# Scoring all four experts in batches 4 and 5 and in one tile of batch 3, with stores on two queues and a new order

## The chip, the cores and the metric

The kernel runs on one core of a Trainium2 chip. The metric is the device time of one execution in microseconds (us), as the median of three runs. Engines are TensorE (PE, with its weight loads PEld), VectorE (DVE), ScalarE (ACT), GpSimd (POOL) and SyncE (SP), which issues the transfers.

## What is computed

The reference has two stages. The first is an attention between x (8 batches, 8 heads, 512 rows, 64 columns) and a state of 32 rows a head, in both directions; its result is a sequence of 544 tokens of 512 columns a batch. The second is a mixture of four attention experts over that sequence, of which each token takes two:

```python
logits = x @ w_gate
topk = np.argpartition(-logits, K, axis=-1)[..., :K]      # K = 2 of E = 4
...
for e in range(E):
    q, k, v = x @ wq[e], x @ wk[e], x @ wv[e]             # 64 columns each
    scores = scale * (q @ k.transpose(0, 2, 1))
    scores = np.where(causal, -1000000000.0, scores)
    scores = scores - scores.max(-1, keepdims=True)
    a = np.exp(scores)
    a /= a.sum(-1, keepdims=True) + 1e-09
    ye = a @ v @ wo[e]
    for kk in range(K):
        mask = topk[:, :, kk] == e
        out += mask[..., None] * w[:, :, kk:kk + 1] * ye
```

## The kernel before

Each float32 operand is split into a high and a low float16 half, and each product is made of three matmuls (high by high, high by low, low by high: `PROD`). The 512 tokens of a batch are four tiles of 128 (`T = 4`); the 32 state tokens of two batches together form a `tail`. For each batch, `front(b)` computes the first stage, the keys, the values, the gate and the queries; `probs(b, unit)` computes scores and exponentials of a unit, which is a list of tiles with a way of scoring; `reads(b, i)` multiplies the probabilities of tile i with the values, weights them, and `result` multiplies with `wo` and stores the tile.

There are two ways of scoring a tile. In the way `"s"` a query tile is multiplied with a mask for each of two slots, so that each slot holds the one expert that its token chose among three; `qf` is the masked query, `qh` its halves, and a DMA transpose turns them into `qm`. A tile then has two lanes of scores of 128*(i+1) columns. In each lane three matmuls have 128 rows of contraction and three have 64; those of 64 rows run in pairs. `reads` makes 194 columns for each slot: three experts of 64 columns and their sums. In the ways `"d"`, `"0"` and `"1"` no mask is used: all four experts are scored, two for each half of the pair index, so a tile has four lanes, and all its matmuls have 64 rows and run in pairs. `"d"` takes both pairs in one unit, `"0"` and `"1"` take one each. `reads` makes 65 columns for each of the four experts. Where all tiles of a batch are of this kind, the queries come out of the matmul already turned and need no mask and no DMA transpose.

For every lane `masked` (DVE) adds the causal mask and takes the row maximum, ACT takes the exponential, and `split` makes the halves `ph`: the high half on ACT, POOL or DVE, the low one on POOL or DVE. A DMA transpose turns `ph` into `pt` for the reads.

Which batch is scored in which way stands in `units_of(b)`:

```python
if b < CFG["D1"]:
    units = [((0, "s"), (1, "s")), ((2, "s"),), ((3, "s"),)]
elif b < CFG["DA"]:
    units = [((1, "d"),), ((0, "s"), (2, "s")), ((3, "s"),)]
else:
    units = [((1, "d"),), ((0, "0"), (2, "0")), ((0, "1"), (2, "1")), ((3, "0"),), ((3, "1"),)]
```

Before, D1 = DA = 6: batches 0 to 5 are scored by `"s"`, batches 6 and 7 by the others. Nothing is issued in program order: each call records a step with the ways (engines) in which it can be done, and `ORDER` holds, in coded form, one order of all steps, the way of each and the slot of each buffer. `run` (line 266 is its issuing line, so nearly all instructions carry L266) issues the steps in that order. The front of a batch is mixed with the scoring and the reads of the batches before it.

Of the kernel before, what the change touches and what calls it, by code (L numbers as in the profile page):

```python
# [18 lines left out]
CFG = dict(FILL=(1.0, 1.4, 1.8, 2.2, 2.6, 3.0, 3.4, 3.8, 4.2, 4.6,), RA=-1, RG=1, RV=2, RK=2, ZL=3, GP=1, PT=4, ZM=4, SM=4, QM=4, SIDE=32, FB=1, PX=1, PA=2, LB=1, xn=4, W0=-33, PACE=37.0, XP=(1,), QP=(0,), LAG=2,
           FRONT=1.5, FSPAN=1.0, TSPAN=1.3, TOFF=1.2, KT=3, p32=3, ph=2, at=1, et=1, gs=1, xh=4, a2=1, o=4, sn=1, qf=2,  # L20
           n_eb=1, n_e2=1, n_a2t=1, n_xt_tail=2, n_z32=3, n_z=2, n_zh=2, n_tq=1, n_tv=2, n_tpt=1, n_tz=1, n_pt=3, D1=6, DA=6)
ORDER = (
    (
        "c-jrs1A7n(7(n6AU$tu4EiBu{vTfV87nW_?wr$(CZR6hGaGvKqfshB%K{iMNksuWmg2<2_GC~oE00kivM1(|;8=^u6%nJYr1PlTS2_X%n$6S"
        "yMazI=Nf|aluih)6V2mps@um%!9bchGBAqFgk<xmb{LUD)#1uzfRfN)S2GC(XSh&ACjlz{S(1xrE&s0AUI6SCq7s0d{s8=izhSQ~O+VMqa$A"
# [3 lines left out]
        "3B%J&h(Tjv2F!v6I1Uy=1X_&?p(HlMdk{dCF(R#pHMj(-;987CO|T{|f~t5Q9zs)m1dZ@DM5e}A3Lii-ERA*XF+73iPz(3-GYF(=_y%r48N3"
        "Z&APPmLJ5Uzy!c%w))$s+C!*}o=YG7*E$F(s#e1MnG4Zp!hsE1#nBi2WwHuwoTqf>Hdj^E)kq=j(Q4(nhi?2bKf9k#_E&;t8mZw$pg*dKpFU"  # L30
        "pxo{uqO`0$v6oA(QgXF!Pp)r;t=eGf2bvPz@ZqEUcq`ChU0M~PC(#E*achREbNL?ur;Ql88{Ua&}<xzKj<$_!<qOC5>jf~fTQvM<Q$8B!yNn"
        "zBQOmG(R7SWV{jz?1H)06mj1w8+=S_9EXJj5G!6mNQyhwk@yHP|5ydCw#551X;ZNF({U|4e$0QUB4?zSBCBmc>8-wX92{UG=WV9V~(>4^`f&"
        "ti{lAvO8%104#0R5tGl!7ARR?I{B={xPfIJgs2QZC9syKo?7q}_M`<KiC7M0sg1=Ag)U7*66o%uE|)5FNxr7)Hv6F$?YG!E_YM(-DlwS;;sW"
# [34 lines left out]
        "c-mc((YB>92tx@_`u~4CJM?%T#-+<@X-Gn<zAGvtZbY2;|58TBgcRp?B#UZSid#xeq}uy=3=%r?9WCklVDfM>Q|$U=XZm%MZHk8fQQ<DZnuY"
        "R~VJ2>KVv1TV8&+yipmpW99!nsW3liFm=wLSQp+nL~b=`;cvd^f|pH6-@pNOM)VO0<>W0$NLbNV@SI+mQj&d5HL1t4eDVd!z+!I4od#`CLj`"
        "mBz89&#-y`*N37M{DiCR~KZvfh-GE+rmb2!c8^l4GIg{2s>*nD~`w4qj76)OqXqZPNJ%8eSd>SV=W!!%7i!;c|bQku*qkeMTK!}rz5}-3ak!"  # L70
        "Uwd%IZn+^F9m|fP-V9H<mvIaIi&}9*Mjb;=xaX{)3)-hUbe9VY_=fhJs#w?gq@@XNm_t)fYI^ml_tGiAbFR+}ohhiNyxeE8}FB?0<No^|Nwu"
        "Y(S{PfF3@^kL<RZ!cS<H);`VcccgJDsyWBcbW-V6NxPuMD3X&yzE8UTWfJ){|6E_CI6E1{V"
# [1142 lines left out]
```

## Time and profile before

| what | value |
| --- | --- |
| median of three runs | 285.18 us (284.17 to 285.38) |
| the profiled execution | 284.73 us |
| its span, from first to last instruction | 283.0 us |
| granted TensorE clock, mean | 0.994 |
| busy, PE / DVE / ACT / POOL | 270.7 / 252.9 / 230.5 / 170.2 us |

The profiled execution has 1.7 us outside the span that the trace shows. Busy times count each engine's own instructions, overlaps once; a mean in nanoseconds counts the whole of one instruction, with the part that overlaps its neighbour.

### The profile page before, as it was taken

The page shows a single profiled execution, that of the slowest core. Times are in us where ns is not written, and L with a number is a line of the kernel's source. Part 1 is how long each engine was busy: PE and PEld are TensorE (multiplying, and loading weights), DVE is VectorE, ACT ScalarE, POOL GpSimd, SP SyncE. Part 2 cuts the span into 40 slices and gives each one's busy share as a digit, 9 for nine tenths or more (in the row PEclk, how much of TensorE's full clock was granted, in tenths as well). Part 3 has the DMA queues.
Part 4 walks back from the last instruction along what each step waited for, and adds up shares of the span by engine and source line. Part 5 has one row for each costly group of instructions (what it writes and reads, how often), then busy time and mean ns, then how long its engine had stood idle before and what let it go on. Part 6 is the DMA issues. An engine that isn't in the chain of part 4 may idle for free.

```text
span 283.0 us, 9152 instructions
## 1 busy us (share of the span) xinstructions
PE 270.7 (96%) x3406; PEld 182.6 (65%) x3407; DVE 252.9 (89%) x795; ACT 230.5 (81%) x624; POOL 170.2 (60%) x246
## 2 busy tenths in 40 slices
PE   8969999998998999989999999999999999999995
PEld 4757665857477664758677756668567575666763
DVE  2588999899999999999999998999998999979962
ACT  3689998899799999778988889796777698869523
POOL 7522556596784897859656974577685842654010
PEclk9979999999999999999999999999999999999999
DMA  7956799999999999995999999998788799699996
GB/s 197 237 107 157 182 195 177 195 218 171 179 173 193 145 186 292 192 201 135 238 197 183 190 201 230 141 203 209 133 152 164 226 147 199 122 184 188 209 227 244
DMA packets 161804, 53.16 MB, mean 188 GB/s; under 512 B 140640, under 2 KB 157280, under 8 KB 161760
## 3 DMA queue, kind: packets, MB, share of 16 engines
q1 hardware_dynamic: 161760, 52.59, 95.0%
q8 instruction: 26, 0.43, 0.6%
q14 instruction: 18, 0.15, 0.2%
HBM read 11.02 MB, written 8.91 MB: 70 GB/s over the span
## 4 chain that ended last, share of the span: by engine, by line
PE 68%; DVE 19%; ACT 6%; issue 3%; DMA 2%; SPq 1%; POOL 0%; DVEq 0%; ACTq 0%
PE bank L266 68%; DMA xn<-in_x_dram 2%; DVE eb L266 2%; DVE xh L266 1%; DVE qf L266 1%; DVE sbm L266 1%; DVE gs L266 1%; DVE mb L266 1%; DVE p L266 1%; DVE z L266 1%; DVE a L266 1%; DVE ph L266 1%; SPq L266 1%; DVE m L266 1%; DVE et L266 1%
## 5 line engine op out<-in xcount | busy, mean ns | idle before, releaser
L266 PE MATMUL bank<-gs,at 128*128 128x260 f16 (+3 forms) x320 | 44.8, 284 | 1.4 <-DVE kt L266 0.8
L266 ACT ACTIVATE p<-p,mx 128x256 f32<-128x256 f32 (+3 forms) x80 | 41.8, 554 | 2.8 <-DVE mx L266 1.7
L266 PE MATMUL bank<-v,pt 128*128 128x194 f16 (+1 forms) x600 | 42.1, 226 | 0.5 <-DVE mx L266 0.4
L266 PE MATMUL bank<-kt,qm 64*128 64x128 f16 (+7 forms) x384 | 42.3, 298 | 0.2 <-DVE kt L266 0.2
L266 PEld LDWEIGHTS <-pt 128*128 128x128 f16 x600 | 38.3, 97 | 5.2 <-issue 2.9
L266 DVE CUSTOM_DVE_ANT_0 p<-bank,band 128x384 f32<-128x384 f32 (+3 forms) x80 | 36.4, 481 | 0.7 <-PE bank L266 0.3
L266 POOL TENSOR_TENSOR ph<-p,ph 128x1024 f16<-128x1024 f32 (+1 forms) x17 | 32.8, 1930 | 5.7 <-ACT ph L266 5.1
L266 PEld LDWEIGHTS <-at 128*128 128x128 f16 x288 | 27.3, 97 | 9.3 <-issue 2.9
L266 PEld LDWEIGHTS <-qm 64*128 64x128 f16 (+1 forms) x384 | 21.0, 95 | 17.1 <-issue 7.6
L266 PE MATMUL bank<-at,gs 128*128 128x512 f16 (+1 forms) x116 | 29.3, 395 | 0.7 <-ACT gs L266 0.7
L266 PE MATMUL bank<-wo_n,z 128*128 128x512 f16 (+1 forms) x114 | 26.2, 368 | 0.0
L266 ACT ACTIVATE ph<-p 128x1024 f16<-128x1024 f32 (+1 forms) x21 | 20.3, 965 | 0.4
L266 POOL TENSOR_TENSOR qh<-qf,qh 128x768 f16<-128x768 f32 x10 | 17.1, 1719 | 4.9 <-ACT qh L266 4.9
L266 PE MATMUL bank<-wo_n,zp 128*128 128x512 f16 x84 | 19.9, 379 | 0.0
L266 ACT ACTIVATE o<-bank 128x512 f32<-128x512 f32 (+1 forms) x27 | 15.4, 575 | 4.9 <-PE bank L266 2.7
L266 DVE SCALAR_TENSOR_TENSOR xh<-xn,xh 128x512 f16<-128x512 f32 x26 | 18.3, 705 | 0.0
L266 POOL TENSOR_TENSOR eb<-eb,sbm 128x512 f32<-128x512 f32 x14 | 15.1, 1077 | 5.1 <-DVE gt L266 2.4
L266 PEld LDWEIGHTS <-gs 128*128 128x128 f16 x108 | 10.2, 98 | 11.5 <-issue 1.1
L266 PEld LDWEIGHTS <-xh 128*128 128x128 f16 x416 | 14.4, 99 | 4.1 <-DVE xh L266 2.1
L266 PEld LDWEIGHTS <-z 128*128 128x128 f16 x114 | 10.3, 98 | 10.1 <-issue 1.1
L266 ACT ACTIVATE gs<-bank 128x260 f16<-128x260 f32 (+3 forms) x32 | 15.2, 499 | 1.1 <-PE bank L266 1.1
L266 ACT ACTIVATE xh<-xn 128x512 f16<-128x512 f32 x24 | 14.7, 629 | 1.2 <-DMA xn<-in_x_dram 1.1
(246 smaller groups left out, 668.2 us busy)
## 6 DMA issues: line engine op xcount, KB each, us to landing
out_dram<-o SPq DMA_DIRECT2D x33, 256.0 KB, 3.0
xn<-in_x_dram SPq DMA_DIRECT2D x14, 512.0 KB, 5.3
xn<-in_x_dram SPq DMA_DIRECT2D x4, 256.0 KB, 3.7
sn<-in_state_dram SPq DMA_DIRECT2D x8, 64.0 KB, 3.9
...
pt<-ph SPq DMA_TRANSPOSE x28, 4.7
...
```

The source lines that it names most:

```text
L266: f(**{k: v.ap() if isinstance(v, View) else v for k, v in kw.items()})
```

## The change

Batches 4 and 5 are scored as batches 6 and 7 are, tile 1 of batch 3 by `"d"`, and tiles 0 and 2 of batch 3 form one unit. A store of an output tile can be begun by ACT as well as by SP. One warming matmul is added at the start (`FILL`, 11 entries instead of 10). The order, the engines and the buffers of all steps are new: the list of steps has 1954 entries instead of 1927. No function is new.

```diff
-CFG = dict(FILL=(1.0, ..., 4.6,), ..., D1=6, DA=6)
+CFG = dict(FILL=(1.0, ..., 4.6, 5.0,), ..., D1=3, DA=4)
...
-    ORDER: three coded strings (steps, ways, slots)
+    ORDER: three other coded strings
...
         return self.step("SP", max(1.18, transfer + 0.35) if transpose else issue, [(f, dict(out=out, in_=in_))], [v for v in (in_,) if isinstance(v, View)],
-                         [v for v in (out,) if isinstance(v, View)], land=transfer, after=after, issue=issue, late=late)
+                         [v for v in (out,) if isinstance(v, View)], land=transfer, after=after, issue=issue, late=late,
+                         ways=None if transpose or not isinstance(in_, View) else [("SP", issue, [(f, dict(out=out, in_=in_))]), ("ACT", 0.35, [(self.nc.scalar.dma_start, dict(out=out, in_=in_))])])
```

## Rows read from the trace of the kernel before

**Rows 1.** Chain that ended last, in time: start, duration, what

```profile
126.55 38.63 PE bank L266 x548
...
243.20 0.61 DVE kt L266
...
243.85 35.85 PE bank L266 x462
```

**Rows 2.** Busy us of PE, PEld, DVE, ACT, POOL, by stretch

```profile
55.00:126.50 71.50, 67.73 (x816) 44.82 (x800) 69.40 (x208) 64.75 (x184) 53.81 (x70) 1.00 1.05 195
126.50:243.90 117.40, 117.08 (x1494) 78.91 (x1495) 111.52 (x363) 98.37 (x276) 78.14 (x98) 1.00 0.95 184
243.90:283.00 39.10, 35.79 (x462) 23.35 (x461) 28.46 (x104) 22.21 (x57) 10.34 (x14) 1.00 0.91 198
...
100.00:120.00 20.00, 19.48 (x223) 12.54 (x221) 19.14 (x56) 17.91 (x46) 16.92 (x20) 1.00 1.15 220
```

**Rows 3.** PE in order of time: start, duration, scores of one or more units

```profile
195.78 1.75 PE L266 MATMUL bank<-kt,qm 128*128 128x128 f16 x24
...
203.57 2.21 PE L266 MATMUL bank<-kt,qm 128*128 128x512 f16 x12
...
213.00 0.83 PE L266 MATMUL bank<-kt,qm 64*128 64x256 f16 x12
...
230.92 1.47 PE L266 MATMUL bank<-kt,qm 64*128 64x512 f16 x12
```

**Rows 4.** Groups by form, whole span: busy us, mean ns, idle before

```profile
L266 PEld LDWEIGHTS <-pt 128*128 128x128 f16 x600 | 38.3, 97 | 5.2 <-issue 2.9 <-DMA pt<-ph 0.2
L266 PE MATMUL bank<-v,pt 128*128 128x194 f16 x360 | 33.3, 247 | 0.5 <-DVE mx L266 0.4
...
L266 PE MATMUL bank<-v,pt 128*128 128x65 f16 x240 | 8.8, 194 | 0.0
```

**Rows 5.** The page's costliest groups, all four widths of a lane together

```profile
L266 ACT ACTIVATE p<-p,mx 128x256 f32<-128x256 f32 (+3 forms) x80 | 41.8, 554 | 2.8 <-DVE mx L266 1.7
...
L266 DVE CUSTOM_DVE_ANT_0 p<-bank,band 128x384 f32<-128x384 f32 (+3 forms) x80 | 36.4, 481 | 0.7 <-PE bank L266 0.3
```

**Rows 6.** DVE groups by form between 126.5 and 243.9 us

```profile
L266 DVE TENSOR_TENSOR z<-bank,c 128x384 f32<-128x384 f32 x10 | 5.5, 547 | 0.3 <-POOL c L266 0.3
...
L266 DVE TENSOR_TENSOR ph<-p,ph 128x1024 f16<-128x1024 f32 x3 | 3.7, 1223 | 0.0
...
L266 DVE TENSOR_TENSOR qf<-bank,m 128x384 f32<-128x384 f32 x6 | 3.2, 540 | 0.0
...
L266 DVE TENSOR_TENSOR z<-z 128x128 f32<-128x128 f32 x8 | 2.8, 348 | 0.0
...
L266 DVE SCALAR_TENSOR_TENSOR qm<-bank,qm 128x512 f16<-128x512 f32 x4 | 2.6, 678 | 0.0
...
L266 DVE TENSOR_TENSOR z<-bank,c 128x256 f32<-128x256 f32 x1 | 0.4, 425 | 0.0
```

**Rows 7.** ACT groups by form between 126.5 and 243.9 us

```profile
L266 ACT ACTIVATE z<-bank,c 128x64 f32<-128x64 f32 x36 | 7.9, 323 | 0.2 <-DVE c L266 0.2
L266 ACT ACTIVATE ph<-p 128x1024 f16<-128x1024 f32 x7 | 7.4, 1057 | 0.2
...
L266 ACT ACTIVATE qh<-qf 128x768 f16<-128x768 f32 x5 | 4.0, 839 | 0.5 <-DVE qf L266 0.5
L266 ACT ACTIVATE qf<-bank,m 128x64 f32<-128x64 f32 x18 | 3.9, 338 | 0.5 <-POOL m L266 0.4
...
L266 ACT ACTIVATE qm<-bank 128x512 f16<-128x512 f32 x4 | 2.4, 591 | 0.4 <-PE bank L266 0.4
```

**Rows 8.** POOL groups by form between 126.5 and 243.9 us

```profile
L266 POOL TENSOR_TENSOR ph<-p,ph 128x1024 f16<-128x1024 f32 x6 | 12.8, 2131 | 0.4 <-ACT ph L266 0.3
L266 POOL TENSOR_TENSOR qh<-qf,qh 128x768 f16<-128x768 f32 x6 | 9.8, 1650 | 2.8 <-ACT qh L266 2.8
```

**Rows 9.** Stores begun by SP, 126.5 to 243.9: issue, min/median/max ns

```profile
L266 SPq DMA_DIRECT2D out_dram<-o x18: 332/572/1523, 137.1 to 238.2; - x18
```

More of the change, by code (lines that the diff above doesn't have):

```diff
@@ L17 @@
 AX = mybir.AxisListType
[L19 removed]
+CFG = dict(FILL=(1.0, 1.4, 1.8, 2.2, 2.6, 3.0, 3.4, 3.8, 4.2, 4.6, 5.0,), RA=-1, RG=1, RV=2, RK=2, ZL=3, GP=1, PT=4, ZM=4, SM=4, QM=4, SIDE=32, FB=1, PX=1, PA=2, LB=1, xn=4, W0=-33, PACE=37.0, XP=(1,), QP=(0,), LAG=2,
            FRONT=1.5, FSPAN=1.0, TSPAN=1.3, TOFF=1.2, KT=3, p32=3, ph=2, at=1, et=1, gs=1, xh=4, a2=1, o=4, sn=1, qf=2,
[L21 removed]
+           n_eb=1, n_e2=1, n_a2t=1, n_xt_tail=2, n_z32=3, n_z=2, n_zh=2, n_tq=1, n_tv=2, n_tpt=1, n_tz=1, n_pt=3, D1=3, DA=4)
@@ L29 @@
[L29 to L33, printed above, removed]
@@ L67 @@
-    (
[L68 to L72, printed above, removed]
+        "c-jTQ17HvU5CFjUXIopg?b=$lZQHh2%eHOXwr$&XcaZ@Afq+3kAs$45Wl#jtLw+a-$sh(qg-j3;@<IlP20@S+3qS%W2AOa<B!uE%kO)>lByf"
@@ new lines @@
+        "lci6J(`hgc8?RzVV21L2??lz;#z533<1RDiUQ8}j1`s0oF!09J&!Pzy>zC8!OhAU77oLYNWqV0g%jr=SQH#e8@YqC;iKj%DC9)PX8+2J%4;y"
+        "Z|}z9MpxXa31nNJ*Wna-~gP3`cM|CLlY<s7ojmUfEsWK0^u^`!d-9$B0vk+3s<2bWWlzu5?aDF$cn9CEd*gF*au3jVI5?{rm!3Kz!umK3vfG"
+        "ZgRRg8y2DOr4$WW(EW}{!0h!@C9EEnU5jw*SD282N32uf(coP<5e@F*opbsp?W!Mw?LSYyHo1g-IrGXHF>){BGg<en*m*XVZ0KK6-^n>Df3="
+        "Y99Sb<5ws00pz<S-b9z)Bnn2caYm1EC1i0fxgo7y*%~6js6sFcKnCHs}gdpc_nt(s&!9(0mAmGB_Ec(m0q3$6*@GfmL`H#=~@|j2&S$*1}OR"
+        "7aHO{xC6Cu0nC7U_=QHpLYN7&pb<u+`q&g3V<f7Bv!M!>#W1Lf%`iGGf^v8t4nuRShUIZFFg3v=um-E+19$`t@C`hK$4~>Gz*AU@&mbn%#3i"
@@ new lines @@
+        "r}pF?+i0kNnqw!oJVgWka_=!tJ(DRjcN*aN%Zdx%XRp(TEW&e#q=Kp#v6{jo2$#{t+6U&BEB1cUH148|eo)C)V{cUX_%s3Q)=R`?Bi<1qXJ!"
+        "|?}%r`fm(N8le~o`fl2ByL9F3HXzy;0BzCzi2Yf!I?M}<IpUehQeL3HU5N9{7us_3C+dC6hMLW3&vntnunus2BxF9^c&*fModrLP`M2zpt1N"
+        "564GCai=#0Sjl=mEj{q}J1xiYY@enyaeIvqu6d(V<cXCXC<M9Xer;0Ry7;_TwKuSg#X%OY3aF~mNAvuL%cuYYNFgF#Xl(YpSVkRmCsVE_4ro"
+        "oh-1QTH)`U|P4042tQxDE5r4opK^QE@wFp}e#cPhnO{f`@SkRiZ-}33p>v8cKWcupGg?7#XvX@i8>aPEjyE@4^V23v$pQPQd#x85SnzVHA!d"
+        "a%7Ig`!Nbf<;rxFk75-{j#04$CFG(MjgMmrEJJ57JRiUSEK8@c8K=Y`O2o}Mm`YMA48$W+j;c{=98Muro~ly|E=EPD2BpE8)RJ3qOFGGCxHi"
@@ new lines @@
+        "?I=v;@=VqJ=fi8%)6gjSReJ5xP6%cZD3oyAie3)|2oZa}3e2b{o$RGdaoC?(-@IGS2hTRO+5xe=YmEYO$&xCxD-^W2`AQb!8p4m6V5QBv+gJ"
+        "?JEMqRW^XE^`?5qGlA6li~%wjTi6=wxEj~i+fURZq3apCHJPQcnz=cSZc%RF%8GzRD2QJa#y;J(J(Hj<<vZm;_)54i<dA1j;CWB9be%Dnn=g"
+        "F8%?4<G?`BD7`n>c=^nnuH<*myVmj_i@9-v1p*wtylXE}1#Tof7r-AF7f^YLwYRA(kJ>THz^d9f=H=IE;DFesA9P*N9(F?xM_i;Aml#G~(4|"
+        "6V=L-{#2e#g_2TXJ(p{(y7o0sp{d^Z+l)PkhB6u@mQ!*Zh!wVI^KcCuAi}*H!d}i^3T>C!cULEvHMenjT_%F2E<{vdp8ra$eTa7CI$)xC7_q"
+        "8(5IHQg&WLH!+`N=A8T+-*SFgPkZPQ{=q`LmTut&+D2J82mi$jl8+y8F0Rb;DToX6WB!c6{Dg~eG2Tm$aXS^|1@w-yatLpveYArXQh6@U@A("
@@ new lines @@
+        "Tp<@%hBD{u+^z>BCh@1(O*lJ`?Z-b4+#6qn($d{oMDb*{=)_#l17YP^dINF)A-&$s~}lN$VmkIM{g%+L9X9H1urk-zd2ti#Xc6My6H{F$HQ9"
+        "VskLxhB`;+j59%@eP@(KRB!0l=*s?>hTM?DnPg71s0TRl1=W)Sz4q=2x);{m!ot~vdbLJB*&<boTHR_oKoq1IYH;?DW=wwlwOL+1xllH^&<V"
+        "`m$I8O$OGxjzxWUT=2!Aip5Y7X#%Z++cju-0S{}(_%`EdYja;Ixyi9v=Po83@=r8x;0sL5c^GoW(S)?z&qRSM<3-vUm)7SKdmTP+L#{>C^q?"
+        "L@4K?m_?8O(2K4FBW)JeJ>)%X>l@$K!bjr;`w1xk7Jb0-vD|)J{ZHNG9@7jw<2B1f+w!m8%p{I>{G_CX+aV#FCNxRbop<jU;g-vb@A_GJ<2s"
+        "5{)Z&=&8JuEZSZ&X>^Gx^X$EJlwmxXhjT-TB3ZSwgz`emtnuWBJd;Lpmm14QY9c>nvfZQKGKzmmSNSFh<b%xAo77Zh=|_n#f25hTkc4udzRM"
@@ new lines @@
+        "?>t*zu5jphf`T)N3aTA?jvz9o{@LiC8HaA{5~k7<o=<6AV9lgKpQt)FN*w~-ARAT#(nt<;&^U7pZw3X}!bTh{A#-lJV)qO8?b+E-@rI_)n3n"
+        "pFD8Y@TiXWC!<<WHLZLQ*znKDWs_E;y~>wlccSz*2%J*gJiF!k{Om%Q_61cB?DzX2g_iYA}iP}wItJUwug(!A`5T(G(=W%a*befc#y2(1-w!"
+        "B@_sEYGwmtO<xN^brs)tVDGPZuC(@y^*h<MFUc;qjj;-ZqG>^;3V&1IJDTOZKX|j)p$x<#W5p9Gd)^ajc%F8UNAS2~~R+PCGU#CkFtt6Etfr"
+        "iR59xnU2ip-JOl29M&IzGUU^q`KCxspw*%4nG(PxP^FQPS+XRgY^VJETuFhaT2v8bP;dF3qW?tm`?qZr8tZLQm;QohPoRb*fd9X%;54Y`#P`"
+        "(J`_^LG$WN$qK54HJmPx=~i7L=|4f;sf#68S4ke-r9m1|Ye-QIuNyc!6w%09Ol!(&iDLOQims6(x>lChLfOdcBt)0UVmiqAb*ZejvRX@)+Gb"
@@ new lines @@
+        "ua<#ep<uw_y}*VqPGE{kNlEwh5U+*VjrTWM=;3-7dXvO=Qk5-Oxeb)~GbT~<<;Qd1o-#r2Do(29CS*I5kvY87<1?U3erOuyL;I<L)if|S?q_"
+        "E$^kMromyG=@giowD9`$pvkvRkgJKu(SG0cS|&@tW|W6RMT@R)<MhYKiw;PY=fcw)>c|wYv@L6sekmUwpX%E7TxZuT1?w)Y&Er`?zK(QN%xu"
+        "AKDn>=^nw1go4Q$|DcF9ysJC^CZIxfP)%Htk-DbD+j&74Ic3FShbG@!@w3cSK&bpQRX>Glsn>dGE(-+!ZV`^6GqS>si9=1AqNn`01&1qdVx5"
+        "d`&a=>cK0jVQB^qAF^H`-I<=n;#n2d$pG)NUG2`|B&sWq+)$zSUlO+zweDJ1D*Nwbs+4Hb4jJJ1uDS<-LB;K?+{lK5Aa8ub;Gt<+BDF%Zl1("
+        "Eo=?7koD30Hdz1KA&G52w6FfNvR2-L?6n130sEp~^_!NlV)o8L?7RNdI9A+7>ky4==q0S2HINDx&%(5w57qeg-V)deOK4Rrk&V&BR@su+SUq"
@@ new lines @@
+        "hYtfW=6aazgFSb)8;jvi<yEvZ$tx7Nl!S}99rojtj=wG`IaQrahLXQ}LkowCoiMcP|6Yic#@rKPqe*2T$d+AC{jEv%8&vhm8^+^Sn`>*N!3q"
+        "_(uiTF07bD~sq|Jyg4S8tdt;t)q!|uwEY7)$3X$zi6E-t#$W$*2kjwW$SDc)qRw9wf271dV5q)XFa@w_i^)B-q*WWKkx5XY=95bzShms+d%J"
+        "bm#m+K^By+H``ch2U>U5nNAoxy-sAajP3m#Iz76r7cHM@0Y#-(~t(Qgc=srS+dv8nWBRtfSd2)~M*Q|}l@Y|NqNBTf(U@1JNC-6Zw$`X61kG"
+        "4^s$ipm^-?6iH!&3V#OXH(`u#K@WPv__Cye09p9^h?#jHmZNAM1I2oHw-be!(XAU7O??e4<bGd-lLGc}9C^_bsE3wSu0{hgfERWaBK874XM4"
+        "#WP!eA8t=<s6DkpUeupi79VfVt*|$;Nt)G*cs8HvL7v@5SPl>N$y&@Sc}_3xm3@L$@enWJ!>p>8^lCmuOZhY(Y14g%&-7eg+Glxnui<4px6k"
@@ new lines @@
+        "&PUd!irS)XWmyqwSVx?bBSSsgF$^}N0}@P^*V=XqnV;7z=uxA6Ji)E9V5Z{^Lrx&H?S=E)5"
+    ),
+    (
+        "c-p0vQ4#|o2t$3`|IqDJR3xzNO!sH4i;$3D$2bq`&G_fBm1r(FiM3SmYonN_&G&4kdt;mMB1rrYUbalRL+nI_I-krbczq`Kg&l-)$ZXju4se"
+        "E|A5E76`Mb?pF)Z-1tL7}bfw0+-Q{qbsGFCw(_d>kD9nM9a#zpdl0*6SFY(enDrSLE!o4}V&$OpdGD{7+<kDgbwau^2b8+w{*iUR+p*Nt|qH"
+        "?7KKwBz0SHkp`gzM>t3naWdgS3Gi}(pGZ*h+j!40N+_Nr+y^}Onjl23ObTJf#box@m3yX$3#+e>Mz2oXJC>#Op+vxE^YHEP=2#Bt&Q`wQ>f`"
+        "JCtZyAW`t^7dKNsO`%k5xpq20ibGQL+"
+    ),
@@ new lines @@
+    (
+        "c-mD{0g}Wp2og2={~sS<?`E!@ZL^7@fZhGB?#POmKumG*@5(?&foJ)KKcFT8K)gt-ma&T2tW<o0d%Sg`5G0J*%nS?|)EUM9+U6;k={NInMe+"
+        "6-A$BslmYqE#5|g!5fZ*#DYcdr_fZMG$Ce@)JiCx#yW5MLw<%`U!>p+hv`9%+w$le3lmdPPq#=(4)%PN=BjL2>%V$}+xS!4BI@FM|2O^Y5o<"
+        ";|lUV+d`<5}23f$1<NZOSSYK?Se{V9D+n;@TN<ZnzDX+$g8Y1yZm)RO4V!3vZXnV73am1CEonJr-mXfG)St<6)+`bQE8+@Y9fRi1g>5QnGcB"
+        "i$v0<|i^zZ4TEEtv>eoY3b%~?_LR;%shk|!1aYQ_X*S?ZRhO8R&Xx!Bky~OU>gD0uXmNUms*&N_c8F_9oZ|>TJ10I=r(l|5=q;3jQm#U5@bp"
+        ">sE_RmV<?4wNU+V)9;#Vqm2!4~%oP<oit4$|th`}z($xn@gLlz1Eg5$wND<NKOUR6)lNNxueQ"
```

35 lines of the change are left out of this document (removed).

## The prediction

> **What bounds the kernel now.** I read the chain that ended last first. From 126.55 us to the end it is PE working without a pause, but for about ten microseconds before 243.85, where it passes through DVE and ends on a `kt` half that PE needs [rows 1]. So the second half of the kernel is PE's, and DVE is next in line. The busy times by stretch say the same in shares. Between 126.5 and 243.9 us, where batches 4 and 5 are scored and read, PE is busy 117.08 of 117.40 us, DVE 111.52 (95%), ACT 98.37 (84%), POOL 78.14 (67%). Between 55 and 126.5 us it is the other way round: DVE 69.40 of 71.50 (97%), and PE 67.73 (95%). In the last 39.10 us DVE has only 28.46 of work and ACT 22.21 [rows 2]. The reader is to see two things. A microsecond taken from PE after 126.5 is worth up to a microsecond, and DVE has but 5.9 us to give before it sets the pace itself.
>
> **What PE saves.** Scores of an `"s"` batch are three units: tiles 0 and 1 (384 columns a lane, 1.75 us), tile 2 (also 384 columns, and taken at the same 1.75) and tile 3 (512 columns, 2.21), in sum 5.71. Scored with four experts, a batch costs 0.83 for tile 1, which is 256 columns twice over, 0.83 for each of two units of tiles 0 and 2, which have the same 512 columns in all, and 1.47 for the two units of tile 3: 3.96 [rows 3]. That is 1.75 less a batch. The reads of a batch are 2 slots x 10 blocks x 3 = 60 matmuls of 194 columns, at 33.3 / 360 = 0.0925 us, 5.55; then 4 x 10 x 3 = 120 of 65 columns at 8.8 / 240 = 0.0367, 4.40 [rows 4]. That is 1.15 less. Two batches give 5.8. For tile 1 of batch 3: scores 0.83 + 2.21 (tiles 0 and 2, 512 columns) + 2.21 against 5.71, 0.46 less; reads 24 x 0.0367 against 12 x 0.0925, 0.23 less. In all PE has 6.5 us less, and 110.9 us is the least that the stretch can take. The query products have the same columns in both ways, 24 matmuls of 256 or 12 of 512, and are taken as equal.
>
> The price of the narrow reads is a row, not an estimate: 0.0367 us each, with weight loads that last 0.097 but overlap [rows 4]. Beside this, the Trainium skill, page "TensorE: Matmul & The Clock Gate", section "Back-to-back issue gap", gives some 81 ns as the sustained spacing of load and matmul pairs at 128 columns; as an estimate from that page of the Trainium skill 240 narrow reads would cost 240 x (0.081 - 0.037) = 10.6 us more than by the row. By that rule the change would cost PE time; the trace disagrees with it, at less than half of the Trainium skill's figure.
>
> **What the other engines gain or lose** (two batches, 8 tiles; shares between engines as the stretch has them).
> DVE: 16 more masked lanes at 36.4 / 80 = 0.455 [rows 5], +7.3; four low halves of queries straight from the bank, 0.65 each (2.6 / 4), +2.6; no masked queries, 6 of 9 of which are DVE's, 5.3 x 0.540, -2.9; the weighting of reads, 8 x 0.425 in place of 5 x 0.547 (10 on DVE to 6 on ACT), +0.7; four of the sums of `z` gone, 4 x 0.348, -1.4 [rows 6]. That is +6.3, and +0.4 for batch 3 (two lanes more, a mask and a sum less): DVE would need 118.2 us.
> ACT: 16 exponentials at 0.554 [rows 5], +8.9; 5120 more columns of `ph`, five high halves at 1.057, +5.3; four query halves at 0.591, +2.4; less 2.7 masked queries of six parts at 0.338, -5.4; 3.3 `qh` at 0.839, -2.8; and three weightings of six parts at 0.323, -5.8 [rows 7]. +2.6, with batch 3 +3.7: 102.1.
> POOL: five low halves of `ph` at 2.131, +10.7, if POOL takes them all; four `qh` at 1.650, -6.6 [rows 8]; 82.2. On DVE such a half costs 1.223 [rows 6].
>
> **Stores, the added matmul, the new order.** A store holds SP 0.572 us in the median, 0.332 at least [rows 9]. What it holds ACT is not shown: between nothing and 18 x 0.572 = 10.3 us, if all go to ACT. I take half of the stores at the smallest row, 3.0, because the choice is free and SP can keep those that hurt. A store of a tile that DVE wrote would make ACT wait, with the exponentials behind it, which DMA transposes and then PE's reads wait for. The 3.0 fit into ACT's 117.4 - 98.4 = 19.0 us of idle time [rows 2]; if DVE's overflow fills that, they cost what they last. The warming matmul lies in the start, before inputs land: nothing, and at most its own duration. The new order ahead of 126.5 us can win or lose: PE is idle 3.8 us between 55 and 126.5 [rows 2], so from -3.8 to about as much the other way. I take nothing, as no row says which. The DMA engines' share falls if at all: a batch loses 48 blocks of `qm` and gains 40 of `pt`.
>
> **The sum.** With PE at 110.9 us, DVE at 97%, its share between 55 and 126.5, has room for 107.6; it must give up 10.6 of 118.2 to ACT and POOL, or the stretch is longer. How densely the three can work is in [rows 2]: 69.40 + 64.75 + 53.81 over 71.50 is 2.63 engines at once, and 19.14 + 17.91 + 16.92 over 20 is 2.70 between 100 and 120 us. The work is 118.2 + 102.1 + 82.2 = 302.5, so 115.0 or 112.0 us. If all 10.6 went from DVE to POOL at 2.131 / 1.223, the work would be 310.4: 118.0 or 115.0. I take 113.5, the middle of the first pair, because where DVE's work goes to ACT it costs no more (0.591 against 0.678 for 512 columns of `qm`, [rows 6, 7]). That is 117.4 - 113.5 = 3.9 less. The profiled execution took 284.73, so 280.8; on the median of the runs, 285.18, it is 281.3. I predict 281.0.
>
> **Rivals.**
> *All of PE's saving comes through* (0.22). Spare time on POOL and ACT and the slack of DVE in the last 39 us take the overflow, or the new order mends the waits before 126.5. For it: POOL is 33% idle. Against: no stretch shows four engines that full. 284.73 - 6.5 = 278.2, and lower if the order wins too.
> *DVE becomes the bound* (0.19), the case on the other side. The place is the masked lanes of batches 4 and 5. With nothing given up, 118.2 at 97% is 121.7 us, +4.3: 289.0; each low half of `ph` that DVE takes adds 1.2. It decides from where DVE keeps more than 0.971 x 117.4 = 114.0, that is gives up less than 4.2. For it: the chain already runs through DVE ahead of 243.85 [rows 1], where batch 6 is scored with four experts. Against: PE stood still only some tenths there.
> *A balance at no gain* (0.13). At 2.63 engines and with the overflow on POOL, the stretch takes 118.0: 285.3.
> *The narrow reads wait for their weights* (0.01). If the 0.097 us of each load [rows 4] lay open, 240 reads would take 23.3 instead of 8.8: PE +14.5 - 6.5, some 293. The Trainium skill's figure above would point to this mechanism. The 240 narrow reads of before, at 0.0367, speak against it.
>
> **How the numbers follow.** The forecast, 279.5 to 283.5, has 0.45. A difference under 0.5% (1.4 us) can't be told from none. Faster by more: 0.45 + 0.22 = 0.67; within: 0.13; slower: 0.20. The range takes the full saving with some of the waits before 126.5, 276.5, and reaches to 287.0, into the case where DVE is the bound; about one in ten is left on either side.
>
> **What would show it.** After the change the reads of batches 4 and 5 are 65 columns wide at about 0.037 us each; there are 98 masked lanes in place of 80 (8 more in each of two batches, two in batch 3); the stretch that scores batches 4 and 5 is shorter by 3 to 5 us, and DVE there is at 96% or more with PE down to 97 to 98%. If PE is still at 99% and the stretch 6 us shorter, the first rival holds. If the chain of waits runs through DVE's masked lanes and PE idles over 8 us, the second does. I would be wrong if ACT, with stores and exponentials, came to 97% and became the bound, or if the new order put new waits ahead of 126.5 us.

## The result, and the profile after

The kernel after takes 287.16 us (median of 17 runs, 284.75 to 290.41), the kernel before 284.54 in the same session: ratio 1.0083, 95% interval 1.0056 to 1.011. It is slower by 0.8%; the forecast was 281.0, and 287.16 lies just outside its range. The profiled execution took 287.38 us, with a span of 285.6.

The mean granted clock of TensorE is not the same in all executions: in the profiles of both kernels it is 0.97 of full speed up to 55 us (PE is for a part of that time at 1.2 instead of 2.4 GHz, having been busy for 8.3 of the first 10 us in the kernel before and 7.5 in the kernel after) and 1.00 from there to 243.9. The kernel before takes 283.5 us in the median where the mean of an execution is 1.00 (47 executions in the sessions of the experiments) and 284.9 where it is 0.99 (95); the kernel after takes 285.7 (6) and 287.0 (8). Where a difference below is of this size, it is given at equal clock too.

From the page of the kernel before, its transfer queue and the chain that ended last by engine:

```profile
q1 hardware_dynamic: 161760, 52.59, 95.0%
...
PE 68%; DVE 19%; ACT 6%; issue 3%; DMA 2%; SPq 1%; POOL 0%; DVEq 0%; ACTq 0%
```

From the page of the kernel after: busy times, two transfer queues, the same chain, and the three groups that answer to [rows 5] and to POOL's halves [rows 8].

```profile
PE 266.3 (93%) x3515; PEld 172.4 (60%) x3516; DVE 250.9 (88%) x810; ACT 233.1 (82%) x612; POOL 181.7 (64%) x260
...
q1 hardware_dynamic: 162592, 46.75, 94.6%
q10 hardware_dynamic: 4032, 7.08, 7.7%
...
PE 31%; DVE 23%; DMA 15%; ACT 14%; POOL 9%; issue 6%; SPq 1%; ACTq 0%; DVEq 0%; POOLq 0%
...
L268 ACT ACTIVATE p<-p,mx 128x256 f32<-128x256 f32 (+3 forms) x98 | 51.1, 558 | 2.0 <-POOL mx L268 1.5
L268 POOL TENSOR_TENSOR ph<-p,ph 128x1024 f16<-128x1024 f32 (+1 forms) x24 | 48.7, 2030 | 4.6 <-ACT ph L268 3.2
L268 DVE CUSTOM_DVE_ANT_0 p<-bank,band 128x128 f32<-128x128 f32 (+3 forms) x98 | 44.0, 480 | 0.8 <-PE bank L268 0.5
```

The work that the prediction counted is there: 98 masked lanes and exponentials in place of 80, PE 4.4 us less busy, POOL 11.5 more, ACT 2.6 more, DVE 2.0 less. What is new is the transfers. The chain that ended last held 2% of DMA before and holds 15% now, and PE's share of it fell from 68% to 31%. Before, one queue had 161760 packets at 95.0%; now two have 166624 and the shares add up to 102.3%. The 4864 packets more are 38 blocks of 128 rows. The second queue is that of the stores begun by ACT, 7.08 MB. That these draw on the same 16 engines as all other transfers is what the Trainium skill says (page "DMA: Bandwidth & Descriptors", section "Issuing engines are not separate DMA queues"). A run below is in keeping with it: without the stores of batches 0 to 6 (e3) the transposes of the other queue land earlier, `pt` in 4.4 instead of 5.3 us.

Windows of the kernel after, columns as in [rows 2] (the last three are PE's clock, the DMA share and GB/s):

```profile
55.00:126.50 71.50, 68.59 (x897) 45.94 (x895) 69.24 (x213) 65.69 (x178) 54.82 (x77) 1.00 1.15 195
126.50:243.90 117.40, 115.47 (x1549) 70.81 (x1548) 110.71 (x376) 102.38 (x266) 87.26 (x105) 1.00 1.07 195
243.90:285.60 41.70, 33.29 (x451) 21.18 (x447) 27.28 (x100) 23.53 (x67) 7.24 (x13) 0.99 0.95 189
```

These windows lie at the same times, but in two orders they do not hold the same work. Beside [rows 2], the DMA share between 126.5 and 243.9 us rose from 0.95 to 1.07. PE is idle 285.6 - 266.3 = 19.3 us of the span, against 12.3 before, and most of the difference stands at the end: 41.70 - 33.29 = 8.4 us idle after 243.9, against 39.1 - 35.79 = 3.3.

A mark of equal work is the last read of batch 5, which is the 360th matmul of `v` by `pt` before and the 492nd after. The matmuls that it ends, before:

```profile
228.81 2.17 PE L266 MATMUL bank<-v,pt 128*128 128x194 f16 x24
```

and after:

```profile
226.30 1.63 PE L268 MATMUL bank<-v,pt 128*128 128x65 f16 x48
```

It ends at 230.98 us before and at 227.93 after: up to there the kernel after is 3.05 us ahead. From the mark to the end, before and after:

```profile
230.98:283.00 52.02, 48.52 (x593) 30.25 (x592) 40.68 (x138) 33.58 (x81) 15.03 (x24) 1.00 0.91 193
```

```profile
227.93:285.60 57.67, 49.21 (x645) 29.89 (x644) 41.97 (x147) 37.25 (x100) 15.76 (x23) 1.00 0.96 184
```

PE has 0.7 us more to do there and ACT 3.7, but it takes 57.7 us instead of 52.0. So the whole loss stands behind batch 5, where batches 6 and 7 are scored in the same way as before.

Groups of the kernel after by form, whole span, answering to [rows 4]:

```profile
L268 PE MATMUL bank<-v,pt 128*128 128x194 f16 x228 | 21.2, 247 | 0.6 <-ACT e L268 0.4
L268 PE MATMUL bank<-v,pt 128*128 128x65 f16 x504 | 17.8, 194 | 1.2 <-DMA pt<-ph 1.2
```

The narrow reads cost 17.8 / 504 = 0.0353 us each, as the row of before had it; both kinds together fell from 42.1 to 39.0 us.

The issues of DMA transposes, with the median us from issue to landing. Before:

```profile
pt<-ph SPq DMA_TRANSPOSE x28, 4.7
...
xT<-xh SPq DMA_TRANSPOSE x24, 3.8
a2t<-a SPq DMA_TRANSPOSE x16, 3.4
...
z<-zh SPq DMA_TRANSPOSE x15, 2.6
qm<-qh SPq DMA_TRANSPOSE x10, 3.8
...
zp<-zhp SPq DMA_TRANSPOSE x7, 3.6
```

and after:

```profile
pt<-ph SPq DMA_TRANSPOSE x32, 5.3
...
xT<-xh SPq DMA_TRANSPOSE x24, 4.7
a2t<-a SPq DMA_TRANSPOSE x16, 3.4
...
z<-zh SPq DMA_TRANSPOSE x15, 4.2
...
zp<-zhp SPq DMA_TRANSPOSE x7, 4.7
qm<-qh SPq DMA_TRANSPOSE x6, 4.9
```

All of these but `a2t` land later, also `xT`, `z` and `zp`, whose number and size did not change. Not each of these steps is clear of scatter. In runs below that keep the order and the transfers of the kernel before (e12, e13, e14, e18), `z` lands in 2.7 to 4.3 us in the median, `xT` in 4.0 to 4.1 and `zp` in 3.3 to 3.5; so the step of `z` proves nothing. Nor is a transpose of 6 us new: behind 243 us the single transposes of `pt` take 4.5 to 6.1 us before and 4.4 to 7.4 after. What is new is that PE waits for them. What waits for them in the last stretch is shown by PE's waits after 243.9 us (total, times, longest):

```profile
PE bank L268 <- ACT tmt L268: 1.3, 1, 1.3
PE bank L268 <- DMA pt<-ph: 1.2, 2, 0.9
PE bank L268 <- DMA tpt<-ptl: 1.1, 1, 1.1
```

and by the chain, in which a transpose of `pt` and one of `tpt` stand after 243 us, where the chain of before is PE without a pause [rows 1]:

```profile
228.21 17.85 PE bank L268 x234
246.06 6.37 DMA pt<-ph
252.51 1.07 ACT ph L268
...
265.28 1.13 SPq L268
266.46 5.06 DMA tpt<-ptl
271.56 10.43 PE bank L268 x104
```

The `pt` transpose is followed by ACT's `ph`: there are two buffers of `ph`, and ACT can fill one only when the transpose out of it has landed.

### The profile page after: what moved, and what is told of

Same layout as the page of the kernel before. It is cut to its first block, busy times and chain, and to the rows that moved or that the text cites. A ratio compares the mean times of both kernels' runs of the same rounds, so it can differ in the third digit from the quotient of the medians.

```text
span 285.6 us, 9384 instructions
## 1 busy us (share of the span) xinstructions
PE 266.3 (93%) x3515; PEld 172.4 (60%) x3516; DVE 250.9 (88%) x810; ACT 233.1 (82%) x612; POOL 181.7 (64%) x260
## 2 busy tenths in 40 slices
DMA packets 166669, 54.42 MB, mean 191 GB/s; under 512 B 145504, under 2 KB 162144, under 8 KB 166624
## 3 DMA queue, kind: packets, MB, share of 16 engines
q10 hardware_dynamic: 4032, 7.08, 7.7%
## 4 chain that ended last, share of the span: by engine, by line
PE 31%; DVE 23%; DMA 15%; ACT 14%; POOL 9%; issue 6%; SPq 1%; ACTq 0%; DVEq 0%; POOLq 0%
PE bank L268 31%; DMA a2t<-a 5%; DMA pt<-ph 5%; DVE p L268 3%; POOL eb L268 3%; DVE ph L268 2%; ACT p L268 2%; DMA z<-zh 2%; DMA tpt<-ptl 2%; DMA xn<-in_x_dram 2%; ACT ph L268 2%; DVE sbm L268 2%; DVE xh L268 1%; DVE gs L268 1%; DVE eb L268 1%
## 5 line engine op out<-in xcount | busy, mean ns | idle before, releaser
L268 ACT ACTIVATE p<-p,mx 128x256 f32<-128x256 f32 (+3 forms) x98 | 51.1, 558 | 2.0 <-POOL mx L268 1.5
L268 POOL TENSOR_TENSOR ph<-p,ph 128x1024 f16<-128x1024 f32 (+1 forms) x24 | 48.7, 2030 | 4.6 <-ACT ph L268 3.2
L268 DVE CUSTOM_DVE_ANT_0 p<-bank,band 128x128 f32<-128x128 f32 (+3 forms) x98 | 44.0, 480 | 0.8 <-PE bank L268 0.5
L268 PE MATMUL bank<-v,pt 128*128 128x65 f16 (+1 forms) x732 | 38.9, 211 | 1.7 <-DMA pt<-ph 1.2
L268 PE MATMUL bank<-gs,at 128*128 128x260 f16 (+3 forms) x272 | 38.4, 287 | 0.4 <-DVE mx L268 0.3
L268 PE MATMUL bank<-at,gs 128*128 128x512 f16 (+1 forms) x140 | 35.4, 393 | 0.3 <-DVE gs L268 0.3
L268 ACT ACTIVATE o<-bank 128x512 f32<-128x512 f32 x25 | 14.6, 594 | 3.1 <-PE bank L268 3.0
L268 ACT ACTIVATE gs<-bank 128x512 f16<-128x512 f32 (+3 forms) x31 | 15.1, 509 | 1.6 <-PE bank L268 1.3
L268 ACT ACTIVATE v<-bank 128x256 f16<-128x256 f32 x39 | 14.1, 385 | 1.0 <-PE bank L268 1.0
L268 POOL TENSOR_TENSOR c<-su,wgt 128x6 f32<-128x6 f32 (+1 forms) x25 | 6.3, 254 | 13.3 <-DVE su L268 12.5
```

Source lines behind the costliest of these rows:

```text
L268: f(**{k: v.ap() if isinstance(v, View) else v for k, v in kw.items()})
```

## The experiments

All ratios are to the kernel before in the same session (284.58 to 284.86 us), with their 95% interval; differences to the kernel after are to its 287.16 us. The first question was where the time after went: to the stores that ACT begins (theory A below), to POOL's halves and full engines (theory C), or to late transposes (theory T). Each edit that helps the kernel after has a control in the kernel before.

**Stores back to SyncE, and the reverse.** In the kernel after all 35 stores are begun by SP:

```diff
-            for f, kw in s["ways"][ways[n]][2]:
+            way = 0 if s["eng"] == "SP" else ways[n]
+            for f, kw in s["ways"][way][2]:
```

> The changed kernel with all 35 stores begun by SP again, in the changed order. Theory T (transfers: the added DMA transposes of probabilities fill the DMA engines, whose share in the stretch from 126 us rises from 0.95 to 1.06, and the last 40 us wait for transposes): the stores still move the same bytes, so within 1 us of the changed kernel, 286 to 288. Theory A (28 stores of 0.34 us hold ACT, and tie its order to the transfers): most of the saving of PE comes through, 281 to 283.5. Theory C (POOL, DVE and ACT are too full in the new order): no change, 286 to 288.

e1: 289.58 us, 1.0171 (1.0135 to 1.0208): slower than the kernel after by 2.4, and outside of all three ranges. Its transposes land in 4.5 (`pt`) and 3.8 us (`xT`) in the median, as in the kernel before, so early landing alone does not make this order fast. In the kernel before the 27 stores of tiles that ACT wrote are begun by ACT:

```diff
-            for f, kw in s["ways"][ways[n]][2]:
+            way = ways[n]
+            if s["eng"] == "SP" and len(s["ways"]) == 2:
+                way = int(any(self.all[a]["ways"][ways[a]][0] == "ACT" for a in s["after"]))
+            for f, kw in s["ways"][way][2]:
```

> The kernel before, in its own order, with the 27 stores of tiles that ACT wrote begun by ACT instead of SP. Theory A: ACT is held by 27 x 0.34 = 9 us and the kernel is 2 to 4 us slower, 286.5 to 288.5. Theories T and C: PE stays the bound in the second half; within 1 us of before, 284 to 285.5.

e2: 287.26 us, 1.0094 (1.0059 to 1.0129), in the range of theory A and not in that of T and C. Beginning stores on ACT helps the order made for it and hurts the order not made for it; it is not by itself the cost of the change. The chain of that run has a late transpose too:

```profile
265.50 7.61 DMA pt<-ph
```

**Fewer transfers.** In the kernel after the stores of batches 0 to 6 are left out:

```diff
+            m = st.dma(out[b, i * P:(i + 1) * P, part], to, 0.73 / cuts)
+            if b < B - 1:
+                st.left_out.add(m)
...
+            if n in self.left_out:
+                continue
```

> The changed kernel, which leaves out the stores of all tiles of batches 0 to 6 (7 of some 54 MB of transfers; those rows of the output are not written). Theory T: the DMA engines' share falls by some 8%, the transposes of probabilities land in 4.7 instead of 5.3 us, and 3 to 6 us are won, 281 to 284. Theory A: the same, as the stores are also gone from ACT; the run with all stores on SP tells the two apart. Theory C: within 1 us of the changed kernel.

e3: 284.19 us, 0.9992 (0.9959 to 1.0025): 3.0 below the kernel after, 0.2 us above the range of theories T and A and far from that of C. This takes away the 256 KB transfers and what their issue costs ACT; the two are not separated here. Then a transfer with no issue on ACT: only the high halves of x are turned in batches 4 to 7, 64 blocks less (the low halves are left out):

```diff
-                turn(..., xT[:, t].rearrange(...), xh[...].rearrange(...), 8, 8)
+                h = 2 if b < 4 else 1
+                turn(..., xT[:, t, :h].rearrange(...), xh[..., :h].rearrange(...), 8 if b < 4 else 4, 8)
```

> The changed kernel, which transposes only the high halves of x in batches 4 to 7 (16 DMA transposes of 4 blocks instead of 8, 64 blocks of 128 x 128 fewer; the low halves stay those of batch 3). The change added 38 such blocks. Theory T: 3 to 7 us faster than the changed kernel, 280 to 284. Theories A and C: within 1 us of it.

e4: 285.33 us, 1.0033 (1.0006 to 1.0061): 1.8 below, between the 3 to 7 of theory T and the 1 of A and C. The 64 blocks are more than the 38 that the change added. Both together:

> The changed kernel without the stores of batches 0 to 6 and with only the high halves of x transposed in batches 4 to 7, both at once. Alone they brought 3.0 and 1.8 us. Theory T (transfers): the two add up, 281.5 to 283, and PE's waits for transposes in the last 40 us are gone. Theory C (POOL, DVE and ACT are too full in the new order): no more than either alone, 284 to 285.5, with PE idle as long as before in the last 40 us, for DVE and ACT.

e5: 284.14 us, 1.0008 (0.9976 to 1.0041), no lower than without the stores alone: that is the range of theory C and a miss of theory T, by which the two gains add. The chain of this run still ends in the same two transposes:

```profile
242.84 5.83 DMA pt<-ph
...
261.44 0.93 SPq L271
262.42 5.15 DMA tpt<-ptl
```

The controls, the same two edits in the kernel before:

> The kernel before, without the stores of batches 0 to 6: the control for the same omission in the changed kernel. Theory T: in the order of before the transfers lie under PE's work, so less is won than the 3.0 us there: 283.5 to 285. If as much or more is won (282 or less), the stores cost both kernels the same, and transfers explain none of the difference.

e6: 284.36 us, 1.0009 (0.9983 to 1.0035).

> The kernel before, which transposes only the high halves of x in batches 4 to 7 (64 blocks fewer): the control for the same omission in the changed kernel, which won 1.8 us. Theory T: the transposes lie under PE's work, within 0.7 us of before, 284 to 285.4. If it wins 1.5 us or more, the omission's gain says nothing on the change.

e11: 285.44 us, 1.0033 (1.0005 to 1.0062). Neither gains anything. Leaving out transfers (in e3 with their issue on ACT) is worth 1.8 to 3.0 us after the change and nothing before it.

**POOL's halves.** In the kernel after half of the columns of the low halves of `ph` in batches 3 to 5 are left out, which takes POOL from 181.7 to 170.6 us:

```diff
-        split(n, ph[:, :n], ph[:, n:2 * n], p32[:, :n])
+        split(n, ph[:, :n], ph[:, n:2 * n], p32[:, :n], n // 2 if 3 <= b <= 5 else None)
```

> The changed kernel, which makes only half the columns of the low halves of the probabilities in batches 3 to 5 (the other half keeps older values; transposes and all else unchanged). It takes some 1 us off each of 13 instructions on POOL or DVE. Theory C: 2 to 4 us faster than the changed kernel, 283 to 285. Theory T: within 1 us of it, 286 to 288.

e7: 286.66 us, 1.0075 (1.0038 to 1.0112): 0.5 below the kernel after, where theory C had 2 to 4 (at a clock of 0.99 it is 1.2, 285.85 against 287.03). POOL's 11 us more are not the main cause.

**More buffers.** From about 180 us the tiles `xn` are free; two of them serve as two more buffers of `ph` (four in all) and two as buffers of `pt` (five), with the order unchanged:

```diff
+        free = [t.rearrange("p h d -> p (h d)").bitcast(F16) for t in self.tags["xn"]]
+        more = dict(ph=list(self.tags["ph"]) + free[:2], pt=list(self.tags["pt"]) + [... for t in free[2:4]])
...
+                    if k > last:
+                        b.slot = more[b.tag][turns[b.tag] % len(more[b.tag])]
```

> The changed kernel, in which the halves of the probabilities (ph) have four buffers instead of two and their transposed form (pt) five instead of three once the inputs of x are all split (from about 180 us; the four input buffers serve for it). ACT waits 4.5 us for transposes to have read ph. Theory T in the form that transposes land late and hold the two buffers: 1.5 to 3 us faster, 284 to 285.5. Theory T in the form that the transfers' rate itself is the limit, and theory C: within 1 us of the changed kernel.

e8: 285.25 us, 1.0031 (0.9998 to 1.0063): 1.9 below the kernel after (1.7 and 2.1 at equal clock), as theory T has it in the form of late transposes that hold the buffers. The chain now has three transposes, one of them out of an added buffer, which goes by the name `xn`:

```profile
246.11 6.17 DMA pt<-ph
...
255.90 4.84 DMA zp<-zhp
260.74 5.44 DMA xn<-ph
```

The wait for a buffer is gone (ACT waited 3.7 us for transposes out of `ph` from 180 us on, and here no more), but transposes still stand in the chain. With the stores of batches 0 to 6 left out as well:

> The changed kernel with four buffers of ph and five of pt from about 180 us, and without the stores of batches 0 to 6. Without the stores alone it took 284.2, and PE then still waited 5 us in the last 40, behind a ph buffer that a transpose had not yet read (5.8 us in the chain). Theory T (late transposes, through the ph buffers and directly, keep PE's saving from coming through): both gone, 280.5 to 282.5. Theory C (POOL, DVE and ACT are too full in the new order): 284, as without the stores alone.

e9: 282.78 us, 0.9950 (0.9922 to 0.9978): 4.4 below the kernel after and 2.0 below the kernel before, 0.3 above the range of theory T. The view lists two waits of PE after 243.9 us:

```profile
PE bank L285 <- DMA tpt<-ptl: 2.0, 1, 2.0
PE bank L285 <- DVE tk L285: 0.7, 1, 0.7
```

The control, the added buffers in the kernel before:

> The kernel before, with the same additional buffers of ph and pt: the control. PE is without a pause from 126 us on, so both theories expect no difference beyond 0.7 us, 284 to 285.4. If it gains 2 us as the changed kernel did, the buffers have nothing to do with the change.

e10: 285.40 us, 1.0031 (1.0006 to 1.0057): no gain. So the two reliefs together are worth 4.4 us after the change, and each alone is worth nothing before it; both together were not run in the kernel before.

**Is a microsecond of PE worth a microsecond?** In the kernel before two of the three products (`PROD[:2]`) are made in the scores and reads of batches 4 and 5, and nothing else changes; the third product is left out:

```diff
-        for m, (a, c) in enumerate(PROD):
+        prod = PROD[:2] if b in (4, 5) else PROD
+        for m, (a, c) in enumerate(prod):
...
-  ... for j in range(i + 1) for a, c in PROD)
+  ... for j in range(i + 1) for a, c in (PROD[:2] if b in (4, 5) else PROD))
```

> The kernel before, which makes two of the three products (not low by high) in the scores and the reads of batches 4 and 5: 72 matmuls fewer, by the rows of before 3.8 us of scores and 3.7 us of reads, some 7.2 us off PE, about what the change takes off, with nothing added on DVE, ACT, POOL or the transfers. If PE alone sets the second half: 277.5 to 279. If DVE, at 111.5 of 117.4 us there, is next at once (at 97% it needs 115.0): 282 to 283. If the order of before gives nothing back at all: 284.8. Theory T says that the change's own PE saving was worth most of this sum and was eaten by the transfers.

e12: 285.86 us, 1.0046 (1.0018 to 1.0075): no gain, and 1 us above even the last of the three values. What was taken off is 6.3 us by the two groups of the page (scores 42.3 to 39.4, reads 42.1 to 38.7) and 4.4 of PE's busy time (270.7 to 266.3). The window of the stretch, and PE's waits from 126.5 us on:

```profile
126.50:243.90 117.40, 112.45 (x1423) 73.88 (x1423) 112.49 (x363) 98.16 (x276) 77.73 (x98) 1.00 0.96 184
```

```profile
PE bank L266 <- DVE z L266: 1.4, 2, 0.8
PE bank L266 <- DMA pt<-ph: 1.3, 1, 1.3
PE bank L266 <- ACT tmt L266: 1.0, 1, 1.0
PE bank L266 <- DVE mx L266: 0.8, 3, 0.3
PE bank L266 <- DVE qf L266: 0.7, 1, 0.7
```

PE is busy 112.45 in place of 117.08 us [rows 2] and uses the difference to wait, for 0.3 to 1.3 us at a time, mostly for DVE. DVE was the first suspect, so the same was done to it: in batches 4 to 7 of the kernel before it makes a quarter of the columns of the low halves of `gs` and `kt`:

```diff
+            if m:
+                lo, src, hi = lo[:, :m], src[:, :m], hi[:, :m]
             dve(n, nc.vector.scalar_tensor_tensor, out=lo, in0=src, ...)
...
+    def cut(b, n):
+        return dict(m=n // 4) if b >= 4 else {}
```

> The kernel before; in batches 4 to 7 VectorE makes only a quarter of the columns of the low halves of gs and kt (left out: the other three quarters). 24 instructions lose about 8 us of VectorE, worked out from 16 of 0.67 us and 8 of 0.41 us; nothing else changes. Theory D, VectorE alone sets the pace: 277 to 281 us. Theory B, TensorE and VectorE are both full and keep each other's pace: 283 to 285. Theory N, neither of them does: 284 to 285.5.

e13: 283.35 us, 0.9942 (0.9921 to 0.9962): 1.5 less, which is theory B's range and too little for theory D. At equal clock it is 0.6 (at 1.00) and 1.2 (at 0.99). The groups of these instructions went from 21.1 to 13.1 us, DVE's busy time fell by 5.9 (252.9 to 247.0). PE stands still nowhere in the stretch:

```profile
126.50:243.90 117.40, 117.40 (x1484) 79.73 (x1477) 106.81 (x369) 98.66 (x280) 78.65 (x100) 1.00 0.95 183
```

If a busy PE were the bound, a cut of PE on top would now count. Both cuts:

> The kernel before with both cuts: two of the three products in the scores and reads of batches 4 and 5 (some 7 us of TensorE), and a quarter of the low halves of gs and kt in batches 4 to 7 (8 us of VectorE). Theory D: as with VectorE's cut alone, within 1 us. Theory B: 278 to 281.5, 3 us or more below either cut alone. Theory N: 283.5 or more.

e14: 283.77 us, 0.9971 (0.9944 to 0.9997): no more than DVE's cut alone, as theory N has it. With this theories D (by e13) and B (by e14) both fall; after e12 I had held one of the two for likely. The window, and the two transposes at the end of its chain:

```profile
126.50:243.90 117.40, 113.31 (x1416) 74.79 (x1406) 107.08 (x372) 98.75 (x280) 79.22 (x100) 1.00 0.96 183
```

```profile
258.93 5.94 DMA pt<-ph
...
266.87 6.25 DMA pt<-ph
```

No engine is over 97% busy there, and the stretch is hardly shorter. DVE's cut in the kernel after, without and with the added buffers:

> The kernel after with VectorE's cut alone (left out: three quarters of the low halves of gs and kt in batches 4 to 7). Theories D and B, VectorE holds back a TensorE that has been relieved: 282 to 285, 2 us or more below the kernel after. Theory T, after the change late transfers alone set the time: 286 to 287.5.

e15: 287.14 us, 1.0075 (1.0047 to 1.0103): nothing, as theory T had it.

> The kernel after with VectorE's cut and with four buffers of ph and five of pt from about 180 us. Theories D and B with late transposes as a second cause: 279 to 282, the two gains add. Theory T: 285 to 286, as with the buffers alone.

e16: 284.29 us, 0.9981 (0.9950 to 1.0013): 1.0 below the buffers alone, in no theory's range, and the two intervals overlap. If DVE's work counts after the change, it does so only where the transposes are relieved, and then little. The last two runs add a relief to both cuts in the kernel before: of the transfers,

> The kernel before with both cuts (two of three products in the scores and reads of batches 4 and 5; a quarter of the low halves of gs and kt in batches 4 to 7) and with the transfers relieved: the stores of batches 0 to 6 left out, four buffers of ph and five of pt from about 180 us. Each relief alone gave the kernel before nothing. Theory F, full transfer engines are the floor under the two cuts: 278 to 281 us. Theory A, ScalarE's queue passes the waits on: 283 to 284.5. Theory O, small waits of all engines on each other in a fixed order: 282 to 284.

e17: 282.27 us, 0.9905 (0.9868 to 0.9942), 1.5 below the two cuts alone (1.6 and 1.7 at equal clock); and of ACT, where the cut of e13 is made before the high half:

```diff
+            if m:
+                lo, src, hi = lo[:, :m], src[:, :m], hi[:, :m]
             act(n, hi, src, scale=f)
```

> The kernel before with both cuts, and ScalarE too makes only a quarter of the columns of the high halves of gs and kt in batches 4 to 7 (left out: the other three quarters; some 6 us of ScalarE). Transfers as before. Theory A: 279 to 281.5 us. Theory F: 283 to 284.5, as without this cut. Theory O: 282 to 284.

e18: 283.12 us, 0.9956 (0.9928 to 0.9984), 0.7 below e14 (0.2 at equal clock). Both lie in theory O's range; e18 is at the edge of theory F's as well, and theory A's 279 to 281.5 is ruled out. The timeline of DVE tells in which part these five runs differ, since the order of instructions is that of the kernel before in all of them (starts in us of the 19th low half of `xh` that DVE makes and of its last low half of `kt`, and the end of the span):

| kernel | `xh` | last `kt` | between | span | `kt` to end |
| --- | --- | --- | --- | --- | --- |
| before | 112.26 | 243.12 | 130.86 | 283.0 | 39.9 |
| e12, less of PE | 112.12 | 242.95 | 130.83 | 284.3 | 41.4 |
| e13, less of DVE | 110.49 | 240.36 | 129.87 | 280.6 | 40.2 |
| e14, less of both | 110.50 | 240.13 | 129.63 | 281.4 | 41.3 |
| e17, both, transfers relieved | 111.43 | 240.95 | 129.52 | 280.6 | 39.7 |
| e18, less of three | 110.29 | 239.37 | 129.08 | 281.3 | 41.9 |

The cuts lie behind 112 us (only e17 has stores left out ahead of it), and most of the 1 to 2 us between the kernels there come from the first 40 us of each profiled execution: up to 55 us the granted clock was 0.97 in before and e12, and 1.00 in the other four. Three kernels with no cut of the engines (e6, e10, e11) have 130.83 to 131.18 between the two marks. Between `xh` and the last `kt` PE's cut is worth 0.0 us, DVE's 1.0, both 1.2, and ACT's on top 0.55. PE does get ahead on the way: its last read of batch 5 ends 118.73 us after that `xh` before and 117.44 in e12, but before the last `kt`, which is DVE's, those 1.3 us are waited away. After `kt`, PE's cut costs 1.5 us (e12) or 1.1 (e14 against e13). The relief of the transfers gives 1.6 back (e17 against e14), and the two late `pt` of the chain above are not in e17's.

## Why the prediction was wrong

**The sum.** The forecast has one term, "That is 117.4 - 113.5 = 3.9 less", for the stretch of batches 4 and 5; what stands behind that stretch was put at nothing, without a reason. Up to the last read of batch 5 the kernel after is 3.05 us ahead, not far from the 3.9. From there to the end it takes 57.7 us instead of 52.0, with 0.7 us more of PE's work. These 5.7 us are what the sum does not have; 5.70 - 3.05 is the 2.65 by which the profiled execution is longer. How much of the first term is luck stays open, because its premise did not hold.

**The bound.** That premise, and the first step that failed, is "A microsecond taken from PE after 126.5 is worth up to a microsecond". It was read from PE busy 117.08 of 117.40 us and from a chain of PE without a pause [rows 1, 2]. Taking 4.4 us of busy time off PE in the kernel before left the length between the marks as it was (130.83 against 130.86), also where PE was busy 117.40 of 117.40 (129.63 in e14 against 129.87 in e13, 0.24 less). A chain of the work that ended last says who was busy last, not that all others had time to spare: DVE stood at 95%, ACT at 84%, in a fixed order, and PE's lead was waited away for them. Nor does a busy PE say that it never waited: a narrow read stands in the trace with 194 ns and takes 37 of busy time [rows 4], so a pause shorter than the rest would show as no idle time; that was not tested. That DVE alone was the bound in PE's place, as I thought after e12, fell with e13 and e14. What the runs show is that neither PE nor DVE sets the pace of this stretch, nor the two together: with ACT's cut on top (e18, where 6.6, 5.5 and 6.1 us of busy time are gone from PE, DVE and ACT) 1.8 us are won. What holds it then was not settled. The small waits of each engine on the others speak for the order itself, but no run changed the order alone, and neither POOL nor SP's queue was relieved.

**The transfers.** The other step is "The DMA engines' share falls if at all: a batch loses 48 blocks of `qm` and gains 40 of `pt`". The working was wrong: 48 is the number for two batches, since `qm` has 6 blocks a tile and 24 a batch. So a batch gains 16 blocks, batch 3 gains 6, and the sum is 38, which are the 4864 packets seen. The stretch of 126.5 to 243.9 already had a DMA share of 0.95 [rows 2]; it went to 1.07, most kinds of transposes landed 0.6 to 1.6 us later in the median, and in the last stretch ACT, and through it PE, waited for them. Relief of buffers and stores gave 4.4 us back (e9): 2.3 ahead of the last read of batch 5, which ends at 225.67 there, and 2.8 of the 5.7 behind it, by the profiled executions. Each relief alone gave the kernel before nothing (e6, e10, e11). No rival had transfers in it. With them relieved, a gain of 2.0 us is left (e9 against before), where the forecast had 3.9. So transfers and buffers are a cause of the loss, but not shown to be the only one: e9 takes away more than the change added (7 MB of stores, and with them ACT's issues), the two reliefs together were not run in the kernel before without the cuts, where e17 gains 1.5 by them on top of the cuts, and ACT's 3.7 us more behind batch 5, which the new order puts there, were not tested.

**What DVE gives up.** "It must give up 10.6 of 118.2 to ACT and POOL" came about in the main: POOL has 11.5 us more over the span, ACT 2.6, DVE 2.0 less. The rival *DVE becomes the bound* did not happen: DVE is at 110.71 of 117.40 in the same stretch, and its cut after the change gave nothing (e15). The density of work, 2.63 to 2.70 engines, was taken too high: DVE, ACT and POOL come to (110.71 + 102.38 + 87.26) / 117.4 = 2.56, against 2.45 before.

**PE's terms.** These were right in size by their groups. Reads fell by 3.1 us (forecast 2 x 1.15 + 0.23 = 2.5) and scores by 3.5 (forecast 2 x 1.75 + 0.46 = 4.0), and a narrow read costs 0.0353 us. PE's busy time as a whole fell by 4.4 (270.7 to 266.3), as other groups show more of it in the new order. The 81 ns of the Trainium skill (page "TensorE: Matmul & The Clock Gate", section "Back-to-back issue gap") are given for 128 columns. The reads here have 65 and take less than half of that, after as before; no row here puts the figure itself to the test.

**Stores.** I took 3.0 us of ACT for half of the stores, hidden in ACT's idle time. ACT begins 28, of 0.339 us in the median, which is 9.5 us. In this order they help: moved back to SP, the kernel is 2.4 us slower (e1). Whether the 3.0 us that leaving them out gives are ACT's or the transfers' was not told apart.

**What would show it.** The marks of lanes and reads came as said, and PE went down to 98%, but DVE to 94% and not to 96% or more. The new order begins the scores of batch 4 at 147.3 us instead of 163.4, so the length of that stretch can't be compared; its end came 3.05 us earlier, in the 3 to 5 that were named. No sign was named for what stands behind it. The two ways to be wrong that were named, ACT at 97% and new waits ahead of 126.5 us, were not it: ACT is at 87%, and PE's idle time ahead of 126.5 us grew by 0.3 us (busy 48.97 to 55 us and 68.59 to 126.5, against 50.10 and 67.73).
